# Folding batch 1 by mirrored rows first, and moving its transforms and the channel-128 transform

## The chip, the cores and the metric

The kernel runs on one core of a Trainium2 chip. The metric is the device time of one execution in microseconds (us), as the median over several executions. Engine names in the profile: PE is TensorE (PEld its weight loads), DVE is VectorE, ACT is ScalarE, POOL is GpSimd, SP issues most DMAs.

## The reference

```
X = fft(x, axis=1); X = fft(X, axis=2); a = X.real          # x: (8, 3008, 256), float32
t = a.reshape(24064, 256)
h = t @ w_in                                                # (256, 2048)
g = where(h > 0, h, exp(min(h, 0)) - 1)
out = g @ w_out                                             # (2048, 256)
```

The weights are given as 64-bit floats, which the kernel turns into float32 itself.

## The kernel before

**The Fourier part.** The real part of a two-dimensional transform of real data is symmetric, so only half of the sequence positions of a batch (1504 columns, plus one middle column done apart at the end) and 129 of the 256 channels are needed. The transform along the channels is folded into the weights at the start (`fold_chunk` builds `Wc` and `Ws`). The transform along the sequence is a matmul with constant matrices (`MC` for batches 0 and 1, `QM` for batches 2 to 7). It is run in four parts per batch: `ri` 0 (cosine, result in `Rr`) or 1 (sine, result in `Ir`), and `kodd` 0 or 1 (even or odd output positions, which fill the first or second half, RUN = 752 columns, of the batch's 1504). Each part has two halves `par` of three matmuls that go to a PSUM bank of their own: the even half is copied (`copy`, on ACT) and unfolded (`unfold`, two DVE sums into `bs`); the odd half is added and subtracted (`plus`, `minus`, DVE) and so written into the ring. `Rr`, `Ir` and `Rb` are rings of 2048 columns.

**Folding x.** Ahead of the sequence transform the rows that share a cosine up to sign are added. For batch 1, x comes as four tiles `L[0]` to `L[3]` of 128 partitions x 6 rows x 256 channels; `L[1]` and `L[2]` hold the rows in mirrored order. `fold_x` (L636) first folds the channels of each tile (channel d with channel 256 - d: sum into `e0` to `e3`, difference into `o0` to `o3`), then adds and subtracts these over the tiles, which gives the four inputs `EO` of the transforms. All of it is GpSimd work in 32 operations of 384 columns (and four copies of 6 columns for channel 0), put one or two to a step in the order of `FOLDS`. Batches 2 to 7 do it the other way round: `mirror_sum` and `half_sum` add rows, then `channel_fold` folds the channels.

**Channel 128.** The one channel that the folds leave out is transformed for all eight batches at once. `load_ext` reads it element by element, `get_ext` reads it back from DRAM into `xs`, `fold_ext` (GpSimd) makes `xe`, `dft_ext` (TensorE, 24 short matmuls) transforms it, `ext_side` (ACT) copies the four results from PSUM into `side` tiles, `ext_unfold` and `ext_rows` (DVE, on 8 partitions) add them up into a row tile `rx`, which is written to DRAM (`r128_dr`). `spread_ext` reads a row of it for a batch into all partitions of the ring `Rb` and into row 127 of `Ir`.

**The main loop.** 47 tiles of 256 columns, each in eight steps over the 2048 hidden values: 376 steps. In step n TensorE runs `mm_P` (four instructions of the profile, `H<-Rr,Wc`) and later `mm_Q` (`H<-Ir,Ws`), both into one bank `H`; between them DVE's `even_part` (E, L1193) reads the bank, adding channel 128, so `mm_Q` waits for E. `h_minus` (L1207) makes the mirrored columns' values; ACT makes the negative parts (`below_plus`, `below_minus`) and their exponentials (`exp_plus`, `exp_minus`); `g_plus` and `g_minus` (L1223) finish the activation one step later, and with `g_plus` the bank H is free. There are three banks H. Then GpSimd forms four sums of G (L548, `sum_1` to `sum_4`) and TensorE multiplies by `w_out` with seven products per step (`mm_X1` to `mm_X3`, into `pA` to `pD`), with the weight sums `WT`. Every eighth step the tile's result is combined (`comb_copy` on ACT; `comb_1`, `comb_2`, `comb_22`, `comb_3` on DVE), transposed (`turn_u`, `turn_v`) and stored.

**What sets the order.** Every action is put on a list with a due time, in units of T = 4.8 us per step: `at(33 * T + 1.46, fn)` is 1.46 us after the start of step 33. The list is sorted by these times and run once, and each engine's instructions stay in that order. The times order the instructions; they don't delay them. `at_dft(step, gap, ...)` places a transform: even half at the end of `step` (4.75), unfold in the next step at 1.0, odd half at the end of `step + gap`, ring writes in the step after that at 1.01. DMAs on the SP queue are not pinned to the list and are arranged by the framework; those that GpSimd issues are pinned.

Some lines that the prediction uses are helpers: L539 is every matmul, L545 every DVE sum of two tensors, L548 every GpSimd sum, L551 every ACT operation.

Of the kernel before, what the change touches and what calls it, by code (L numbers as in the profile page):

```python
# [9 lines left out]
FP = mybir.dt.float32  # L10
# [152 lines left out]
def kernel(  # L163
# [466 lines left out]
    def fold_x(L, engine_of, cuts_of):  # L630
# [44 lines left out]
        op("EO3", O[3], O[0], O[2], ALU.add)  # L675
        return [E[1], E[3], O[1], O[3]], ops

    FOLDS = (
        "e0 c0 e3 c3 e2 c2 x1 e1 c1 E0 E2 EO0 o0 o3 o2 o1 O0 O2 EO2 EO1 EO3".split()
    )  # L680

    def lines(j, far):

# [437 lines left out]
    def ext_rows(kodd, tt, rows=NB):  # L1121
        n = NO if kodd else NE
        if not kodd or rows < NB:
            rx = spool.tile([128, HALF + 1], FP, tag="rx", bufs=1, name="rx")
            state["rx"] = rx[0:rows]
        rx, a, b = state["rx"], state["es"], state["side", 1][0:rows]
        o, base = 1 - kodd, kodd * RUN
        m = n - 2 * o
        tt(rx[:, base : base + n], a[:, 0:n], b[:, 0:n], ALU.add)
        top = base + RUN - 1  # L1130
        tt(rx[:, top : top - m : -1], a[:, o : o + m], b[:, o : o + m], ALU.subtract)
        if not kodd:
            tt(rx[:, HALF:], a[:, 0:1], b[:, 0:1], ALU.subtract)
            nc.sync.dma_start(
                out=r4_dr.rearrange("o b -> b o"), in_=rx[:, HALF : HALF + 1]
            )
        nc.sync.dma_start(
            out=r128_dr[0:rows, base : base + RUN], in_=rx[:, base : base + RUN]
        )

    def spread_ext(b, kodd):
        for sl, a, z in ring_cut(b * HALF + kodd * RUN, RUN, False):
# [373 lines left out]
    def at(t, fn):  # L1516
        events.append((t, len(events), fn))
# [248 lines left out]
        at_half(step, d, 0, 0)  # L1766
        at_half(step + gap, d, 1, b * HALF + (kodd + 1) * RUN)

    def begin_folds(b):
        state["EO"], state["ops"] = fold_x(  # L1770
            state["L"], lambda key: nc.gpsimd, lambda key, n: (0, n // 2, n)
        )

    steps_b = HALF * 8 // TW
    at(9 * T + 4.75, dft_ext_0)
# [5 lines left out]
    for n in range(16):  # L1781
# [2 lines left out]
            (14.4 + 0.5 * n) * T,  # L1784
            lambda j=j, k=k: load_ext(j, 192 * k, 192 * (k + 1)),
        )
    at(30.0 * T, get_ext)
    at(32 * T + 1.35, fold_ext)
    at(32 * T + 4.75, dft_ext)
    at(33 * T + 1.46, lambda: ext_side(0))  # L1790
    at(33 * T + 1.47, lambda: ext_side(1))
    at(35 * T + 0.2, lambda: ext_unfold(0, vtt))
    at(35 * T + 1.5, lambda: ext_rows(0, vtt))
    at(35 * T + 4.75, lambda: ext_side(2))
    at(35 * T + 4.76, lambda: ext_side(3))
    at(36 * T + 0.2, lambda: ext_unfold(1, vtt))
    at(36 * T + 1.5, lambda: ext_rows(1, vtt))
    at(27 * T + 4.3, quarter_table)
    at(34 * T, lambda: nc.sync.dma_start(out=twist_tab[0:96], in_=QT_dr.ap()))
    for n in range(4):  # L1800
# [1 line left out]
            (51 + 3 * n) * T,  # L1802
            lambda n=n: load_quarter_mats(n % 2, n // 2),
        )
    fold_keys = [(k, p) for k in FOLDS for p in range(2 if k[0] not in "cx" else 1)]
    first = (6, 7, 7, 8, 9, 9, 10, 10, 12, 15)

    def fold_slot(n):
        return first[n] if n < len(first) else 17 + n - len(first)

    at(fold_slot(0) * T, lambda: begin_folds(1))
    n = 0
    for key in fold_keys:
        slot = fold_slot(n)
        at(
            slot * T + (3.5 if slot < 16 else 1.3),
            lambda key=key: state["ops"][key](),
        )
        n += key[0][0] not in "cx"
    for n, (ri, kodd) in enumerate(((0, 0), (1, 0), (0, 1), (1, 1))):  # L1820
        at_dft(
            (28, 36, 40, 44)[n], 2, 1, ri, kodd, lambda k=2 * ri + kodd: state["EO"][k]
        )
    for kodd, step in ((0, 37), (1, 40)):
        at(step * T + 1.0, lambda kodd=kodd: spread_ext(1, kodd))

    def at_quarter(step, b, ri, kodd, finish, join):
# [24 lines left out]
    for b in range(2, NB):  # L1852
# [4 lines left out]
            at((r0 + step) * T + dt, lambda: fn(*key))  # L1857

        for far, rows in (
            (0, ((0, 2, 0.2), (1, 2, 1.3), (3, 3, 0.2), (2, 3, 1.3))),  # L1860
            (1, ((0, 27, 1.3), (1, 25, 0.2), (3, 28, 1.3), (2, 26, 3.0))),
        ):
            for j, n, dt in rows:
                rel(n, dt, load_quarter, b, j, far)
# [83 lines left out]
```

## Time and profile before

| | |
|---|---|
| median of 3 runs (lowest to highest) | 1920.8 us (1920.65 to 1921.17) |
| the profiled execution: its own time | 1921.02 us |
| its span on the core | 1919.1 us |
| PE busy | 1909.2 us (99%), 9008 instructions |
| DVE busy | 1436.9 us (75%) |
| ACT busy | 872.3 us (45%) |
| POOL busy | 1356.9 us (71%) |
| TensorE clock granted | 1.00 |

How to read it: a float32 matmul stands as two instructions. Matmuls are pipelined, so PE's records overlap: consecutive ones over 256 columns start 0.216 us apart though one lasts 0.38. A step of 22 such instructions takes 4.75 us, and where it takes longer without more matmuls, TensorE has waited. Steps are counted from 0 by their first `H<-Rr,Wc`; step 0 starts at 26.57 us, step 36 at 224.35. In the windows view each row is one stretch of the span, with the busy time of each engine in it. In the timeline a row is one instruction or several alike in sequence, with start and length, and in brackets how long the engine stood idle and what ended that.

### The profile page before, as it was taken

The numbers are of one execution on the slowest core, as the hardware profiler recorded it, in microseconds if no ns is written. First come the engines' busy times: TensorE is split into PE (matmuls) and PEld (weight loads), VectorE is DVE, ScalarE is ACT, GpSimd is POOL, SyncE is SP. The second block draws the span as 40 slices with busy tenths as digits, with TensorE's granted clock in tenths as the row PEclk, the third lists the DMA queues.
The fourth block names the chain that finished last, engine by engine and source line by source line (L and its number), as shares of the span: only waits on it lengthen the run. The fifth ranks groups of instructions, "written<-read, shape, count | busy, mean of one in ns | idle before, by whom it ended". The sixth has DMA issues, their size and how long they took to land.

```text
span 1919.1 us, 27636 instructions
## 1 busy us (share of the span) xinstructions
PE 1909.2 (99%) x9008; PEld 1653.4 (86%) x9008; DVE 1436.9 (75%) x2714; ACT 872.3 (45%) x1710; POOL 1356.9 (71%) x1843
## 2 busy tenths in 40 slices
PE   9999999999999999999999999999999999999999
PEld 6788788888888888888888888888888888888887
DVE  8866767877778777777777777777777777667666
ACT  5654444444444444444444444444444444444443
POOL 4888767786687766777667776687766876556565
PEclk9999999999999999999999999999999999999999
DMA  8146112111011110211101111022110210000101
GB/s 338 44 33 52 35 41 53 40 22 33 12 44 37 27 34 12 51 30 31 26 19 45 34 28 26 12 52 43 25 20 12 53 22 15 16 12 14 21 11 24
DMA packets 271073, 71.88 MB, mean 37 GB/s; under 512 B 256815, under 2 KB 257731, under 8 KB 270929
## 3 DMA queue, kind: packets, MB, share of 16 engines
q1 hardware_dynamic: 257296, 57.34, 15.0%
q0 software_dynamic: 11456, 12.52, 2.2%
q8 instruction: 71, 1.16, 0.3%
q14 instruction: 74, 0.60, 0.1%
q10 hardware_dynamic: 2176, 0.26, 0.1%
HBM read 45.20 MB, written 24.80 MB: 36 GB/s over the span
## 4 chain that ended last, share of the span: by engine, by line
PE 96%; DVE 1%; POOL 1%; ACT 0%; DMA 0%; issue 0%; DVEq 0%; POOLq 0%
PE H L539 38%; PE pB L539 17%; PE pC L539 17%; PE pD L539 16%; PE pA L539 9%; POOL WT L548 1%; DMA xl<-in_x_dram,ix 0%; POOL w L548 0%; DVE e L636 0%; ACT G L551 0%; DVE pow L407 0%; DVE o L636 0%; DVE E L1193 0%; DVE G L1223 0%; DVE G L1207 0%
## 5 line engine op out<-in xcount | busy, mean ns | idle before, releaser
L548 POOL TENSOR_TENSOR G<-G 128x256 f32<-128x256 f32 x1440 | 1045.6, 735 | 508.6 <-DVE G L1223 341.9
L551 ACT ACTIVATE G<-H 128x512 f32<-128x512 f32 x376 | 224.5, 597 | 936.5 <-DVE G L1207 931.7
L1193 DVE SCALAR_TENSOR_TENSOR E<-Rb,wex,H 128x256 f32<-128x256 f32 x752 | 328.0, 477 | 376.7 <-PE H L539 371.9
L539 PE MATMUL H<-Ir,Ws 128*128 128x256 f32 x1504 | 387.2, 380 | 2.0 <-DVE E L1193 2.0
L539 PE MATMUL H<-Rr,Wc 128*128 128x256 f32 x1504 | 387.8, 380 | 0.8 <-DVE Ir L545 0.8
L539 PE MATMUL pC<-G,WT 128*128 128x256 f32 x1440 | 369.5, 379 | 0.0
L539 PEld LDWEIGHTS H<-Ir,Ws 128*128 128x128 f32 x1504 | 278.0, 189 | 51.1 <-DVE E L1193 5.6
L539 PEld LDWEIGHTS H<-Rr,Wc 128*128 128x128 f32 x1504 | 282.1, 190 | 44.1 <-issue 2.2
L539 PEld LDWEIGHTS pC<-G,WT 128*128 128x128 f32 x1440 | 273.6, 190 | 37.2
L1207 DVE SCALAR_TENSOR_TENSOR G<-E,H 128x512 f32<-128x512 f32 x376 | 257.0, 684 | 44.6 <-POOL G L548 11.9
L1223 DVE SCALAR_TENSOR_TENSOR G<-G,H 128x512 f32<-128x512 f32 x376 | 255.9, 681 | 40.1 <-ACT G L551 40.1
L1223 DVE SCALAR_TENSOR_TENSOR G<-M,G 128x512 f32<-128x512 f32 x376 | 256.8, 683 | 0.4 <-ACT M L551 0.4
L551 ACT ACTIVATE G<-G 128x512 f32<-128x512 f32 x376 | 233.4, 621 | 0.0
L539 PE MATMUL pD<-G,w 128*128 128x256 f32 x784 | 229.3, 379 | 0.0
L539 PE MATMUL pB<-G,w 128*128 128x256 f32 x784 | 229.3, 379 | 0.0
L539 PE MATMUL pA<-G,w 128*128 128x256 f32 x784 | 229.3, 379 | 0.0
L551 ACT ACTIVATE M<-G 128x512 f32<-128x512 f32 x376 | 224.3, 596 | 3.1 <-DVE G L1207 3.1
L551 ACT ACTIVATE M<-M 128x512 f32<-128x512 f32 x376 | 221.1, 588 | 0.1
L539 PE MATMUL pB<-G,WT 128*128 128x256 f32 x720 | 214.5, 379 | 0.4 <-POOL G L548 0.3
L539 PE MATMUL pD<-G,WT 128*128 128x256 f32 x720 | 214.1, 379 | 0.0
L539 PEld LDWEIGHTS pA<-G,w 128*128 128x128 f32 x784 | 148.9, 190 | 20.5
L539 PEld LDWEIGHTS pD<-G,w 128*128 128x128 f32 x784 | 149.0, 190 | 20.3
(178 smaller groups left out, 1540.1 us busy)
## 6 DMA issues: line engine op xcount, KB each, us to landing
out_dram<-ot SPq DMA_DIRECT2D x496, 32.0 KB
xq<-in_x_dram SPq DMA_DIRECT2D x12, 384.0 KB
out_dram<-ot SPq DMA_DIRECT2D x256, 2.0 KB
xq<-in_x_dram SPq DMA_DIRECT2D x12, 320.0 KB
Rb<-r SPq DMA_DIRECT2D x10, 376.0 KB
raw<-in_moe_w_in_dram SPq DMA_DIRECT2D x7, 512.0 KB
MC<-dft_mats SPq DMA_DIRECT2D x3, 943.5 KB
xl<-in_x_dram SPq DMA_DIRECT2D x4, 512.0 KB
```

The source lines that it names most:

```text
L539: nc.tensor.matmul(out_, lhsT=lhsT, rhs=rhs, start=start, stop=stop, skip_group_check=True)
L548: pin(nc.gpsimd.tensor_tensor(out=o, in0=a, in1=b, op=op))
L551: pin(nc.scalar.activation(out=o, in_=i, func=func, **kw))
L1193: nc.vector.scalar_tensor_tensor(out=S.E[:, c], in0=Rb[:, cols(i)], scalar=wex[:, f : f + 1], in1=S.H[:, c], op0=ALU.mult, op1=ALU.add,)
L1207: nc.vector.scalar_tensor_tensor(out=two(S.G[:, 0:512])[:, :, ::-1], in0=two(S.E), scalar=2.0, in1=two(S.H), op0=ALU.mult, op1=ALU.subtract,)
L1223: nc.vector.scalar_tensor_tensor(out=o, in0=e, scalar=-1.0, in1=h, op0=ALU.add, op1=ALU.max)
```

## The change

- `mirror_folds` takes the place of `fold_x` for batch 1 (batch 0 still uses `fold_x`). It first adds the mirrored rows in place (`L[3]` with `L[2]`, `L[0]` with `L[1]`; each 6 operations of 255 columns and one of 6), then forms sum and difference of `L[0]` and `L[3]` over the freed tiles `L[1]` (kodd 0) and `L[2]` (kodd 1), 4 operations of 384 columns each, and folds the channels of these two, 4 operations of 384 columns each. That is 30 GpSimd operations in place of 36. Channel 0 comes by one ACT copy per `kodd` (`edge`).
- Two to five folds are put in each of the steps 6 to 9; the last is in step 30, where it was 38. The copy of one row from `L[0]` to `L[1]` on ACT comes in step 7 in place of 10.
- Channel 128: `get_ext`, `fold_ext`, `dft_ext` three steps sooner. The two `ext_side` copies for kodd 0 are in step 30 (before 33), those for kodd 1 in step 33 (before 35). `ext_rows(0)` becomes `ext_up` and `ext_down`; the sums are due at 4.25 of steps 30, 31 and 32 (before 0.2 and 1.5 of step 35), those for kodd 1 at 4.25 of steps 53 and 54 (before 0.2 and 1.5 of step 36). `spread_ext(1, 0)` is in step 33 (before 37), `spread_ext(1, 1)` in step 55 (before 40).
- Batch 1's four transforms start in steps 26, 34, 37, 42 (before 28, 36, 40, 44).
- For batch 2 the first load of `xq2` is in step 31 (before 29), since `L[2]` is in use longer.

```diff
--- before.py
+++ after.py
@@ -675,9 +675,60 @@
         op("EO3", O[3], O[0], O[2], ALU.add)
         return [E[1], E[3], O[1], O[3]], ops
 
-    FOLDS = (
-        "e0 c0 e3 c3 e2 c2 x1 e1 c1 E0 E2 EO0 o0 o3 o2 o1 O0 O2 EO2 EO1 EO3".split()
-    )
+    def mirror_folds(L):
+
+        ops = []
+        rows = [t.rearrange("p (m d) -> p m d", d=ND) for t in L]
+        for j, k in ((3, 2), (0, 1)):
+            own, other = rows[j], rows[k][:, ::-1]
+            for m in range(6):
+                ops.append(
+                    lambda own=own, other=other, m=m: gtt(
+                        own[:, m, 1:], own[:, m, 1:], other[:, m, :0:-1], ALU.add
+                    )
+                )
+            ops.append(
+                lambda own=own, other=other: gtt(
+                    own[:, :, 0:1], own[:, :, 0:1], other[:, :, 0:1], ALU.add
+                )
+            )
+        EO = [None] * 4
+        for kodd in range(2):
+            z = L[1 + kodd]
+            for n in range(4):
+                c = slice(384 * n, 384 * n + 384)
+                ops.append(
+                    lambda z=z, c=c, kodd=kodd: gtt(
+                        z[:, c], L[0][:, c], L[3][:, c],
+                        ALU.subtract if kodd else ALU.add,
+                    )
+                )
+            for ri in range(2):
+                t = EO[2 * ri + kodd] = spool.tile(
+                    [128, 768], FP, tag=f"{'eo'[ri]}{1 + 2 * kodd}", bufs=1, name="eo"
+                )
+                for h in range(2):
+
+                    def fold(z=rows[1 + kodd], t=t, ri=ri, h=h):
+                        src = z[:, 3 * h : 3 * h + 3]
+                        lo, hi = (
+                            v.rearrange("p m (d o) -> p m o d", o=2)
+                            for v in (src[:, :, 1:129], src[:, :, 255:127:-1])
+                        )
+                        o = t[:, 384 * h : 384 * h + 384]
+                        o = o.rearrange("p (m o d) -> p m o d", o=2, d=64)
+                        if ri:
+                            gtt(o, lo, hi, ALU.subtract)
+                        else:
+                            gtt(o, lo[:, :, ::-1], hi[:, :, ::-1], ALU.add)
+
+                    ops.append(fold)
+                if not ri:
+                    o = t.rearrange("p (m o d) -> p m o d", o=2, d=64)
+                    state["edge", kodd] = lambda o=o, z=rows[1 + kodd]: act(
+                        o[:, :, 0, 63:64], z[:, :, 0:1]
+                    )
+        return EO, ops
 
     def lines(j, far):
 
@@ -1137,6 +1188,25 @@
         nc.sync.dma_start(
             out=r128_dr[0:rows, base : base + RUN], in_=rx[:, base : base + RUN]
         )
+
+    def ext_up():
+        rx = state["rx"] = spool.tile(
+            [128, HALF + 1], FP, tag="rx", bufs=1, name="rx"
+        )[0:NB]
+        a, b = state["es"], state["side", 1][0:NB]
+        vtt(rx[:, 0:NE], a, b[:, 0:NE], ALU.add)
+        vtt(rx[:, HALF:], a[:, 0:1], b[:, 0:1], ALU.subtract)
+
+    def ext_down():
+        rx, a, b = state["rx"], state["es"], state["side", 1][0:NB]
+        vtt(
+            rx[:, RUN - 1 : RUN - 1 - (NE - 2) : -1],
+            a[:, 1 : NE - 1], b[:, 1 : NE - 1], ALU.subtract,
+        )
+        nc.sync.dma_start(
+            out=r4_dr.rearrange("o b -> b o"), in_=rx[:, HALF : HALF + 1]
+        )
+        nc.sync.dma_start(out=r128_dr[0:NB, 0:RUN], in_=rx[:, 0:RUN])
 
     def spread_ext(b, kodd):
         for sl, a, z in ring_cut(b * HALF + kodd * RUN, RUN, False):
@@ -1766,10 +1836,9 @@
         at_half(step, d, 0, 0)
         at_half(step + gap, d, 1, b * HALF + (kodd + 1) * RUN)
 
-    def begin_folds(b):
-        state["EO"], state["ops"] = fold_x(
-            state["L"], lambda key: nc.gpsimd, lambda key, n: (0, n // 2, n)
-        )
+    def begin_folds():
+        L = state["L"]
+        state["EO"], state["ops"] = mirror_folds(L)
 
     steps_b = HALF * 8 // TW
     at(9 * T + 4.75, dft_ext_0)
@@ -1784,17 +1853,18 @@
             (14.4 + 0.5 * n) * T,
             lambda j=j, k=k: load_ext(j, 192 * k, 192 * (k + 1)),
         )
-    at(30.0 * T, get_ext)
-    at(32 * T + 1.35, fold_ext)
-    at(32 * T + 4.75, dft_ext)
-    at(33 * T + 1.46, lambda: ext_side(0))
-    at(33 * T + 1.47, lambda: ext_side(1))
-    at(35 * T + 0.2, lambda: ext_unfold(0, vtt))
-    at(35 * T + 1.5, lambda: ext_rows(0, vtt))
-    at(35 * T + 4.75, lambda: ext_side(2))
-    at(35 * T + 4.76, lambda: ext_side(3))
-    at(36 * T + 0.2, lambda: ext_unfold(1, vtt))
-    at(36 * T + 1.5, lambda: ext_rows(1, vtt))
+    at(27.0 * T, get_ext)
+    at(29 * T + 1.35, fold_ext)
+    at(29 * T + 4.75, dft_ext)
+    at(30 * T + 1.46, lambda: ext_side(0))
+    at(30 * T + 1.47, lambda: ext_side(1))
+    at(30 * T + 4.25, lambda: ext_unfold(0, vtt))
+    at(31 * T + 4.25, ext_up)
+    at(32 * T + 4.25, ext_down)
+    at(33 * T + 1.46, lambda: ext_side(2))
+    at(33 * T + 1.47, lambda: ext_side(3))
+    at(53 * T + 4.25, lambda: ext_unfold(1, vtt))
+    at(54 * T + 4.25, lambda: ext_rows(1, vtt))
     at(27 * T + 4.3, quarter_table)
     at(34 * T, lambda: nc.sync.dma_start(out=twist_tab[0:96], in_=QT_dr.ap()))
     for n in range(4):
@@ -1802,26 +1872,21 @@
             (51 + 3 * n) * T,
             lambda n=n: load_quarter_mats(n % 2, n // 2),
         )
-    fold_keys = [(k, p) for k in FOLDS for p in range(2 if k[0] not in "cx" else 1)]
-    first = (6, 7, 7, 8, 9, 9, 10, 10, 12, 15)
-
-    def fold_slot(n):
-        return first[n] if n < len(first) else 17 + n - len(first)
-
-    at(fold_slot(0) * T, lambda: begin_folds(1))
-    n = 0
-    for key in fold_keys:
-        slot = fold_slot(n)
+    first = (6, 6, 7, 7, 7, 7, 7, 8, 8, 8, 9, 9, 9, 9, 12, 15)
+
+    at(6 * T, begin_folds)
+    at(7 * T + 3.4, lambda: act(state["L"][1][0:1, 5 * ND :], state["L"][0][0:1, 0:ND]))
+    for n in range(30):
+        slot = first[n] if n < len(first) else n + 1
         at(
             slot * T + (3.5 if slot < 16 else 1.3),
-            lambda key=key: state["ops"][key](),
+            lambda n=n: state["ops"][n](),
         )
-        n += key[0][0] not in "cx"
-    for n, (ri, kodd) in enumerate(((0, 0), (1, 0), (0, 1), (1, 1))):
-        at_dft(
-            (28, 36, 40, 44)[n], 2, 1, ri, kodd, lambda k=2 * ri + kodd: state["EO"][k]
-        )
-    for kodd, step in ((0, 37), (1, 40)):
+    for kodd, slot in ((0, 20), (1, 28)):
+        at(slot * T + 4.0, lambda kodd=kodd: state["edge", kodd]())
+    for step, ri, kodd in ((26, 0, 0), (34, 1, 0), (37, 0, 1), (42, 1, 1)):
+        at_dft(step, 2, 1, ri, kodd, lambda k=2 * ri + kodd: state["EO"][k])
+    for kodd, step in ((0, 33), (1, 55)):
         at(step * T + 1.0, lambda kodd=kodd: spread_ext(1, kodd))
 
     def at_quarter(step, b, ri, kodd, finish, join):
@@ -1857,7 +1922,7 @@
             at((r0 + step) * T + dt, lambda: fn(*key))
 
         for far, rows in (
-            (0, ((0, 2, 0.2), (1, 2, 1.3), (3, 3, 0.2), (2, 3, 1.3))),
+            (0, ((0, 2, 0.2), (1, 2, 1.3), (3, 3, 0.2), (2, 5 if b == 2 else 3, 1.3))),
             (1, ((0, 27, 1.3), (1, 25, 0.2), (3, 28, 1.3), (2, 26, 3.0))),
         ):
             for j, n, dt in rows:
```

## The prediction

> **What bounds the kernel now.** I read the page's busy shares first, then its chain, then the windows step by step, and last the timeline where steps are too long.
>
> ```profile
> PE 1909.2 (99%) x9008; PEld 1653.4 (86%) x9008; DVE 1436.9 (75%) x2714; ACT 872.3 (45%) x1710; POOL 1356.9 (71%) x1843
> PE 96%; DVE 1%; POOL 1%; ACT 0%; DMA 0%; issue 0%; DVEq 0%; POOLq 0%
> ```
>
> TensorE is busy all the time and is the chain. The change removes no matmul (the program's TensorE list has 4312 rows before and after), so it can only win back TensorE's waits. To see those I cut the span where each step's first `H<-Rr,Wc` starts, since a pipelined busy figure hides short waits:
>
> ```profile
> core 0: us, PE busy (x) PEld busy (x) DVE busy (x) ACT busy (x) POOL busy (x), PEclk, DMA share, GB/s
> ...
> 180.16:186.19 6.03, 6.03 (x30) 5.18 (x28) 3.57 (x7) 2.81 (x6) 5.59 (x7) 1.00 0.64 72
> ...
> 209.20:214.05 4.85, 4.85 (x24) 4.26 (x23) 2.35 (x5) 2.32 (x5) 3.22 (x6) 1.00 0.31 90
> 214.05:218.53 4.48, 4.17 (x20) 3.23 (x19) 4.38 (x9) 2.12 (x4) 4.32 (x7) 1.00 0.00 0
> 218.53:224.35 5.82, 5.77 (x27) 4.72 (x26) 5.82 (x11) 2.12 (x4) 4.36 (x7) 1.00 0.01 2
> 224.35:232.52 8.17, 6.64 (x29) 5.12 (x29) 7.48 (x13) 3.91 (x8) 6.79 (x9) 1.00 0.23 38
> ...
> 248.67:254.94 6.27, 6.27 (x29) 5.11 (x28) 4.14 (x7) 3.20 (x6) 5.82 (x9) 1.00 0.01 1
> ...
> 293.24:298.19 4.95, 4.95 (x24) 4.10 (x22) 4.87 (x9) 2.80 (x6) 4.58 (x7) 1.00 0.00 0
> 298.19:302.94 4.75, 4.75 (x24) 4.16 (x23) 3.75 (x7) 2.25 (x6) 3.28 (x6) 1.00 0.00 0
> 302.94:306.82 3.88, 3.88 (x19) 3.40 (x18) 3.67 (x8) 1.71 (x4) 2.99 (x4) 1.00 0.14 22
> 306.82:312.43 5.61, 5.61 (x27) 4.94 (x26) 4.24 (x8) 3.08 (x7) 5.09 (x7) 1.00 0.16 55
> ```
>
> A plain step takes 4.75 us. One followed by the even half of a transform takes 6.03 (step 28, first row), so that half costs 1.28. The rows from 209.20 are steps 33 to 36, then 40, then 48 to 51. Against undisturbed steps of their kind:
> - Steps 33 to 35 take 4.85 + 4.48 + 5.82 = 15.15, where 49 to 51 take 4.75 + 3.88 + 5.61 = 14.24: 0.91 over. 0.10 of it is the change of shape after the narrow channel-128 matmuls. Lost: 0.81.
> - Step 36: 8.17 - 6.03 = 2.14.
> - Step 40: 6.27 - 6.03 = 0.24. Step 48: 4.95 - 4.75 = 0.20.
>
> Together 3.39 us. No other step from 18 to 60 is long. The timeline names the holders:
>
> ```profile
> 216.70 1.13 PE L539 MATMUL H<-Ir,Ws 128*128 128x256 f32 x4 [0.31 <-DVE E L1193]
> ...
> 221.30 2.31 DVE L545 TENSOR_TENSOR rx<-bs,side 8x377 f32<-8x377 f32 x3
> ...
> 223.54 0.67 DVE L1223 SCALAR_TENSOR_TENSOR G<-G,H 128x512 f32<-128x512 f32 x1
> ...
> 226.62 0.70 PE L539 MATMUL pB<-G,WT 128*128 128x256 f32 x2 [0.30 <-POOL G L548]
> ...
> 227.64 0.85 DVE L1193 SCALAR_TENSOR_TENSOR E<-Rb,wex,H 128x256 f32<-128x256 f32 x2
> ...
> 228.54 1.13 PE L539 MATMUL H<-Ir,Ws 128*128 128x256 f32 x4 [1.23 <-DVE E L1193]
> ```
>
> In steps 35 and 36 the channel-128 sums (`rx<-bs,side`, `bs<-side`) stand between `even_part` and `g_plus`. VectorE is then full (5.82 of 5.82, 7.48 of 8.17): `g_plus` gives its PSUM bank back at 224.21, just before step 36's first matmul, the E that `mm_Q` needs comes 1.23 late, and the G sums on GpSimd make one product wait. The first row is another loss: in step 34 `mm_Q` waits for an E queued behind two combination sums.
>
> **What the Trainium skill says.** "TensorE: Matmul & The Clock Gate" (The mechanism): matmuls start and end in program order. The trace agrees: no later matmul passes the one waiting until 228.54, so a late input costs its whole wait. "SBUF — State Buffer" (Who interferes with whom): a VectorE operation with two SBUF inputs contends with a GpSimd operation that reads SBUF. The trace agrees: `rx<-bs,side` over 377 columns takes 1.25 us on 8 partitions, where `Rr<-bs,H`, one input in PSUM, takes 0.54 on 128. I therefore price moved sums at contended durations.
>
> **The change, part by part.**
> 1. *Channel-128 sums.* In quiet steps (30, 38) VectorE runs E from 1.06 to 1.94 us after the step's start, `g_plus` to 2.53, `g_minus` to 3.14, `h_minus` 3.28 to 3.97. The next E is due at 4.75 + 1.06 = 5.81, so the pause is 1.84. Contended prices from steps 35 and 36: step 30 gets the unfold, 1.30; step 31 gets 1.25 + 0.14 (no overlap) = 1.39; step 32 gets 1.06; step 53 gets 1.14 to 1.30; step 54 gets 1.54 to 1.60. All fit with 0.24 or more to spare; the two half sums of step 46, 1.37 long, sit in the same place without loss. Cost 0, and none of it has further cover: past 5.81 each us is a us on TensorE. Removing them from 35 and 36 gives back 2.14 and the 0.21 that step 36's first matmul waited for its bank: **-2.35**.
> 2. *The ACT copies.* `ext_side(0)` and `(1)`, 0.95, move to step 30, behind a transform of 2.1 us; ACT is idle there. `ext_side(2)` and `(3)`, 0.98, come to 33T + 1.46, exactly where 0 and 1 were, behind `comb_copy`, which waits for TensorE until 1.60. So `exp_plus`, `g_plus`, `h_minus` and the two combination sums run as late as now, and step 34's wait stays: **0** gained of its 0.58. Were the copies free there: -0.58; if more is late: +0.3.
> 3. *Transforms.* Their matmuls cost the same wherever they stand. The ring writes (1.06 to 1.13 us) leave step 39 for 37, and 47 for 45, so `h_minus` ends at 3.97 instead of 4.70 ahead of the half sums, and these no longer push E in steps 40 and 48: **-0.44**. In 37, 40 and 45 the writes end `h_minus` by 4.8, as in 31 now, with nothing behind them.
> 4. *GpSimd.* Out: 16 folds from x (10.0 + 9.4 us), 16 pair folds (8.1 + 8.0), 4 copies (1.0), 36.5 in all. In: 12 mirrored sums at 0.735 (the row `xq<-xq,xq`) 8.8, two edges 0.4, 8 sums at about 1.0, 8 folds at about 1.2, together 26.8. Its relief in steps 31 to 38 is what lets the G sums be early; TensorE's 0.57 for that wait is already inside the 2.14. In steps 7 to 9 it carries up to 1.2 us more than now, but its weight pairs are finished some 4 us ahead of `fold_chunk`, and it idles 0.88 at 97.08: 0, bounds -0.3 and +0.5. The two edges on ACT (6 columns) have no row; the nearest is the copy of the same shape on GpSimd, 0.24: idle ACT hides it, at worst +0.3.
> 5. *Queues.* On SP the three early and one late reads of `xs` now go ahead of or around the `xq0` load, which waits for GpSimd's last use of `xl0` in step 26. The last read is issued at 182.84 now. GpSimd needs it at step 29 + 2.0, which is near 190 (step 29 begins 1.9 later than now, with 3.2 of transforms before it instead of 1.3). 2048 packets at the present rate need some 3 us: about 4 us of slack, cost 0. The indirect load of `xq2` on the POOL queue moves from step 29 to 31; 0.94 of issue either way, landing in 4 to 5 us there now, read two steps later. Had it the 11.5 us of other stages, GpSimd would wait 1.5 and TensorE up to 1. The row writes and broadcasts run three steps sooner for half 0 and at step 55 for half 1, needed in 40 and 64.
>
> Sum: -2.35 - 0.44 = -2.79. The profiled execution took 1921.02 (span 1919.1), so 1918.2; the median of the runs is 0.2 lower, 1920.8, so 1918.0. For tenths lost anew I take 0.1 back: **1918.1**. That is 0.14%, inside the 0.2% (3.8 us) a measurement of this kernel can tell from no change.
>
> **Rivals.**
> - *The pauses are too short.* For: margins of 0.24 to 0.8, and contended durations scatter (0.55 to 0.95 for one half sum). Against: the half sums fit. If the five steps each push E by 0.4 plus 0.1 of restart, 2.5 comes back: 1920.4.
> - *GpSimd waits for channel 128* (the slower case). If the last read lands late, `fold_ext` blocks GpSimd at step 29 and four G sums queue behind it, for which TensorE waits. The sums have about 2 us to spare, so it decides from a landing near 192 on, one us for each us. Slower by 0.2% takes 2.8 + 3.8 = 6.6 us more, near 199. For: single-element packets fill the DMA engines until about 178 (share 0.7 to 1.07). Against: two loads of 384 KB leave that stretch. At a landing near 200: 1925.5.
> - *Step 34's wait goes too*, and the 0.36 at 134.3 where GpSimd's weights are late: 1917.2.
> - *Nothing moves*, because the instruction order stayed: excluded for VectorE, whose list has the sums in 30 to 32 and 53 to 54; if the waits have another cause, 1920.8.
>
> **How the numbers follow.** Forecast case, 1917.4 to 1918.9: 0.65. Short pauses or an unmoved wait, 1918.9 to 1920.9: 0.20. Step 34 too: 0.05. Slower: 0.10, nearly all past 0.2%. Range 1917.2 to 1920.6. Faster by over 0.2% means below 1917.0; the 3.39 found plus 0.36 come to 3.75, just short of it, so 0.03. Slower 0.09, same 0.88.
>
> **What would show it.** Right: step 36's `H<-Ir,Ws` has no wait, the first matmul of step 36 follows at once, steps 40 and 48 take their kind's time, while `H<-Ir,Ws` of step 34 still waits 0.3 for E. Wrong: waits of TensorE for E in steps 31 to 33 or 54 to 55, for G sums in 29 to 31 (then look at `xs`), or a stretch before 140 us that has changed by over half a us.

## The result, and the profile after

The changed kernel takes **1918.03 us** (median of 22 runs, 1917.18 to 1919.11), where the kernel before takes 1920.80 (22 runs on the same chip). The ratio is 0.9985, with a 95% interval of 0.9979 to 0.9992. So it is faster by 2.8 us, 0.14%, less than the 0.2% that the prediction set as its bound.

One step boundary after the other, the two profiled executions differ like this:

| stretch | before, us | after, us | difference |
|---|---|---|---|
| start to step 18 | 132.31 | 131.60 | -0.71 |
| steps 18 to 59 | 218.10 | 215.41 | **-2.69** |
| steps 60 to 374 | 1550.98 | 1550.87 | -0.11 |
| from step 375 | 17.72 | 17.61 | -0.11 |

Together that is 3.62 of span (1919.1 to 1915.5), and 3.76 of time (1921.02 to 1917.26). The profiled execution of the changed kernel is one of its fastest, 0.8 below its median; that of the kernel before is 0.2 above its own. The difference of the medians is 2.77, so the first row needs care; it comes back at the end of the experiments. Its 0.25 before step 0 is no gain: among the profiles of all runs step 0 starts anywhere from 26.0 to 26.8.

The page's busy shares and its chain have hardly moved, except that TensorE's share is now rounded to 100%:

```profile
PE 1908.1 (100%) x9008; PEld 1654.2 (86%) x9008; DVE 1433.0 (75%) x2714; ACT 872.7 (46%) x1712; POOL 1349.7 (70%) x1837
PE 97%; POOL 1%; DVE 1%; DMA 0%; ACT 0%; issue 0%; DVEq 0%; POOLq 0%
```

The instructive view is again the windows by step, of the changed kernel. The rows are steps 30, 33 to 36, 40 and 48:

```profile
core 0: us, PE busy (x) PEld busy (x) DVE busy (x) ACT busy (x) POOL busy (x), PEclk, DMA share, GB/s
...
194.22:199.07 4.85, 4.85 (x25) 4.26 (x23) 3.54 (x7) 2.80 (x6) 3.01 (x4) 1.00 0.14 21
...
208.56:213.31 4.75, 4.75 (x23) 4.16 (x22) 2.20 (x5) 2.79 (x6) 2.40 (x5) 1.00 0.42 105
213.31:219.21 5.90, 5.59 (x25) 4.19 (x24) 5.36 (x10) 2.53 (x5) 4.67 (x8) 1.00 0.19 61
219.21:224.82 5.61, 5.61 (x27) 4.94 (x26) 3.90 (x8) 2.67 (x7) 4.24 (x7) 1.00 0.00 0
224.82:231.48 6.66, 6.66 (x30) 5.30 (x29) 3.38 (x6) 3.50 (x7) 4.86 (x7) 1.00 0.32 54
...
248.89:253.63 4.74, 4.74 (x23) 4.15 (x22) 3.58 (x7) 0.07 (x1) 1.16 (x2) 1.00 0.32 92
...
290.04:294.79 4.75, 4.75 (x24) 4.16 (x23) 4.03 (x8) 2.12 (x5) 3.80 (x6) 1.00 0.00 0
```

Step 36 now carries the odd half of a transform, which costs 1.90 (steps 28 and 39 of the same kind take 6.65 too), and loses nothing: its PE column is as long as the row. VectorE, which filled 5.82 and 7.48 us in steps 35 and 36, is busy for 3.90 and 3.38. Steps 40 and 48 take their plain 4.75. Step 30 has the 0.10 of the change of shape after the narrow matmuls, which step 33 had before. The one step from 19 to 59 that still waits is 34. It should take 3.88 + 1.28 (the even half that now follows it) = 5.16 and takes 5.90: 0.74 lost, where it lost 0.60 before.

The sums now lie where the prediction put them. This is VectorE's timeline of the changed kernel in steps 30 to 32, which start at 194.22, 199.07 and 203.82:

```profile
198.20 1.22 DVE L545 TENSOR_TENSOR bs<-side 8x189 f32<-8x189 f32 x2
200.13 0.87 DVE L1263 SCALAR_TENSOR_TENSOR E<-Rb,wex,H 128x256 f32<-128x256 f32 x2 [0.71 <-PE H L539]
...
202.95 1.22 DVE L545 TENSOR_TENSOR rx<-bs,side 8x377 f32<-8x377 f32 x2
204.88 0.87 DVE L1263 SCALAR_TENSOR_TENSOR E<-Rb,wex,H 128x256 f32<-128x256 f32 x2 [0.71 <-PE H L539]
...
207.70 0.60 DVE L545 TENSOR_TENSOR rx<-bs,side 8x375 f32<-8x375 f32 x1
```

After each sum E begins 1.06 after its step's start, and VectorE has stood idle for 0.71 before it, waiting for TensorE and not the reverse. And this is the loss that stayed, in the timeline of step 34 (starts at 213.31; the first two rows are the ACT copies and the exponential of step 33):

```profile
210.46 0.98 ACT L551 ACTIVATE side<-H 8x376 f32<-8x376 f32 x2
211.34 0.61 ACT L551 ACTIVATE G<-G 128x512 f32<-128x512 f32 x1
...
211.99 0.69 DVE L1293 SCALAR_TENSOR_TENSOR G<-G,H 128x512 f32<-128x512 f32 x1 [1.48 <-ACT G L551]
...
214.58 0.69 DVE L545 TENSOR_TENSOR v<-u,pC 128x512 f32<-128x512 f32 x1
...
215.18 0.86 DVE L1263 SCALAR_TENSOR_TENSOR E<-Rb,wex,H 128x256 f32<-128x256 f32 x2
...
216.10 1.13 PE L539 MATMUL H<-Ir,Ws 128*128 128x256 f32 x4 [0.31 <-DVE E L1263]
```

It is a chain of five links: the copies `side<-H` hold back the exponential on ACT, this holds back `g_plus` (1.48 idle), so all later VectorE work of step 33 is late, the combination sums run into step 34, E follows them without a pause, and TensorE waits for E.

### The profile page after: what moved, and what is told of

Same layout as the page of the kernel before. It is cut to its first block, busy times and chain, and to the rows that moved or that the text cites. A ratio compares the mean times of both kernels' runs of the same rounds, so it can differ in the third digit from the quotient of the medians.

```text
span 1915.5 us, 27634 instructions
## 1 busy us (share of the span) xinstructions
PE 1908.1 (100%) x9008; PEld 1654.2 (86%) x9008; DVE 1433.0 (75%) x2714; ACT 872.7 (46%) x1712; POOL 1349.7 (70%) x1837
## 4 chain that ended last, share of the span: by engine, by line
PE 97%; POOL 1%; DVE 1%; DMA 0%; ACT 0%; issue 0%; DVEq 0%; POOLq 0%
PE H L539 38%; PE pB L539 17%; PE pC L539 17%; PE pD L539 17%; PE pA L539 9%; POOL WT L548 1%; DMA xl<-in_x_dram,ix 0%; DVE e L636 0%; POOL w L548 0%; DVE o L636 0%; POOL G L548 0%; POOL xl L548 0%; PE M L539 0%; DVE v L545 0%; ACT G L551 0%
## 5 line engine op out<-in xcount | busy, mean ns | idle before, releaser
L539 PEld LDWEIGHTS pB<-G,w 128*128 128x128 f32 x784 | 148.9, 190 | 20.4 <-PE H L539 0.2
```

Of the source, the lines that this page charges most:

```text
L539: nc.tensor.matmul(out_, lhsT=lhsT, rhs=rhs, start=start, stop=stop, skip_group_check=True)
```

## The experiments

Unless said otherwise "steps 18 to 59" is the length of that stretch in the profiled execution (218.10 before, 215.41 after), and each run's ratio is to the kernel before on the same chip (1920.8 to 1921.02). The changed kernel, run again beside some of them, took 1917.92.

### Which part of the change is worth what

**The second half's sums alone.** The kernel before, with only these moved:

```diff
-    at(36 * T + 0.2, lambda: ext_unfold(1, vtt))
-    at(36 * T + 1.5, lambda: ext_rows(1, vtt))
+    at(53 * T + 4.25, lambda: ext_unfold(1, vtt))
+    at(54 * T + 4.25, lambda: ext_rows(1, vtt))
-    for kodd, step in ((0, 37), (1, 40)):
+    for kodd, step in ((0, 37), (1, 55)):
```

> The kernel before, with one change: the channel-128 sums of the second half are due at 4.25 of steps 53 and 54 instead of 0.2 and 1.5 of step 36, and spread_ext of that half follows in step 55. Folds, transforms and the first half stay. Theory 1 (step 36 loses its time to its own sums): the wait of H<-Ir,Ws in step 36 (1.39 with its restart) goes, what is left there is the 0.3 to 0.6 for the bank and for G: 1919.2 us, steps 18 to 60 in 216.5 us. Theory 2 (the sums of step 35 keep E of step 36 late anyhow): 1920.3 or above, 217.5 us or more.

It took 1919.25 (13 runs, 1918.96 to 1919.69; ratio 0.9992, interval 0.9984 to 1.0001), steps 18 to 59 in 216.55. The row of step 36 in the windows, and the waits that the timeline of TensorE still names in steps 34 to 36:

```profile
224.55:231.22 6.67, 6.37 (x28) 5.19 (x29) 4.93 (x9) 4.18 (x8) 6.43 (x9) 1.00 0.26 43
```

```profile
216.90 1.13 PE L539 MATMUL H<-Ir,Ws 128*128 128x256 f32 x4 [0.32 <-DVE E L1193]
226.82 0.70 PE L539 MATMUL pB<-G,WT 128*128 128x256 f32 x2 [0.30 <-POOL G L548]
```

Step 36 falls from 8.17 to 6.67. The wait of 1.23 for E is gone, and what is left is what the first half's sums in step 35 leave behind: 0.28 for the bank at the step's first matmul (0.21 of it in step 35's row) and 0.57 for a G sum. A bracket says less than a wait costs: it counts from the end of the record before, which lasts 0.38 where the next could start after 0.216, so 0.16 more is lost; and the second matmul after a wait starts 0.32 later instead of 0.216, 0.10 more. 0.30 in the bracket is 0.57 of loss, and the 1.23 were 1.49. So these two edits are worth 1.5 of the 2.8 us, and step 36 lost its time to its own sums. The interval of the ratio includes 1 (its end is 1.0001); it is the trace that places the gain. Not all of the 1.49 was the length of the sums. In the kernel before, the unfold of step 36 also waited for the ACT copies that it reads, and E stood behind it:

```profile
226.56 1.14 DVE L545 TENSOR_TENSOR bs<-side 8x188 f32<-8x188 f32 x2 [0.54 <-ACT side L551]
```

**The fold alone.** `mirror_folds`, its slots and the later load of `xq2` are put into the kernel before, with the transforms in 28, 36, 40 and 44 and channel 128 where it was:

```diff
-    for step, ri, kodd in ((26, 0, 0), (34, 1, 0), (37, 0, 1), (42, 1, 1)):
+    for step, ri, kodd in ((28, 0, 0), (36, 1, 0), (40, 0, 1), (44, 1, 1)):
...
+    at(35 * T + 0.2, lambda: ext_unfold(0, vtt))
+    at(35 * T + 1.5, lambda: ext_rows(0, vtt))
```

> The mirrored-row fold alone: transforms in steps 28, 36, 40, 44 and the channel-128 work at the old times. Theory 1 (the place of the channel-128 sums in steps 35 and 36 costs the time; GpSimd's relief alone cannot move E of step 36): step 36 still takes about 8.1 us; 1920.0 to 1920.8, less only by what the start gives (step 12, 0.57 in the one profile). Theory 2 (GpSimd was the cause, its folds in steps 29 to 38 made the G sums late and contended with VectorE's sums): step 36 falls to near 6.1; 1918.5.

It took 1920.76 (13 runs, 1919.80 to 1922.83; ratio 1.0, interval 0.9991 to 1.0008). Its profiled execution, 1919.80, is its fastest; steps 18 to 59 take 217.27 in it. There the waits for G and for the bank are gone, and E's is not; step 36 takes 7.58, between the 8.1 and the 6.1 of the two theories:

```profile
223.20:230.78 7.58, 6.36 (x29) 5.04 (x28) 6.35 (x12) 4.26 (x8) 5.41 (x9) 1.00 0.23 39
```

```profile
226.81 1.13 PE L539 MATMUL H<-Ir,Ws 128*128 128x256 f32 x4 [1.22 <-DVE E L1263]
```

The row sums of step 35 took 1.51 there instead of 2.31. But the fold alone gains nothing that the runs can show. The 0.83 of its profiled execution is more than its median supports (0.26 below the kernel before on that chip, with runs that scatter over 3 us), and I don't use it.

**The old fold in the changed kernel.** `mirror_folds` is taken out again (`fold_x` and its 36 operations in the old slots), and all else stays as changed.

> Changed kernel, but batch 1 folded in the old way, in 36 GpSimd operations up to step 38. Theory 1: VectorE's places give the time, so steps 33 to 48 stay as in the changed kernel apart from at most 0.6 of waits for G sums; step 12 loses its 0.57 again; 1918.0 to 1919.0. Theory 2: GpSimd is over-full in steps 29 to 38 again, and 2 us or more come back: 1920 or more.

It took 1918.21 (21 runs, 1917.67 to 1919.58; ratio 0.9986, interval 0.9979 to 0.9992), steps 18 to 59 in 215.45: within 0.04 of the changed kernel. With the rest moved, the new fold is not needed for the gain in these steps. In steps 29 to 38 no TensorE wait for a G sum came back either, although GpSimd has its old load.

**The later transforms back.** The three later transforms are put back:

```diff
-    for step, ri, kodd in ((26, 0, 0), (34, 1, 0), (37, 0, 1), (42, 1, 1)):
+    for step, ri, kodd in ((26, 0, 0), (36, 1, 0), (40, 0, 1), (44, 1, 1)):
```

> Changed kernel with the last three transforms of batch 1 at their old steps (36, 40, 44; the first stays in 26). My theory (ring writes in steps 39 and 47 end h_minus late, ahead of half sums that then push E in 40 and 48): steps 40 and 48 take 6.27 and 4.95 again, 0.44 more, 1918.5. Rival (those two were after-effects of the crowded steps 35 and 36): both stay undisturbed, 1918.0.

It took 1918.65 (21 runs; ratio 0.9988, interval 0.9981 to 0.9994), steps 18 to 59 in 215.91, which is 0.50 more than as changed. Steps 40 and 48 are long again, to within a hundredth, and make 0.43 of it:

```profile
246.02:252.29 6.27, 6.27 (x29) 5.11 (x28) 4.14 (x7) 3.20 (x6) 5.82 (x9) 1.00 0.01 1
...
290.59:295.53 4.94, 4.94 (x23) 4.10 (x22) 4.86 (x9) 2.79 (x6) 4.57 (x7) 1.00 0.00 0
```

**Step 34's wait.** In the changed kernel the two copies are put after the exponentials of step 33:

```diff
-    at(33 * T + 1.46, lambda: ext_side(2))
-    at(33 * T + 1.47, lambda: ext_side(3))
+    at(33 * T + 2.3, lambda: ext_side(2))
+    at(33 * T + 2.31, lambda: ext_side(3))
```

> Changed kernel, with ext_side(2) and (3) due at 33T + 2.3 instead of 33T + 1.46, so that ACT does exp_plus and exp_minus of the step first. My theory (the two copies of 0.98 us ahead of exp_plus make g_plus, h_minus and the two combination sums late, and step 34's H<-Ir,Ws waits for E): that matmul no longer waits, 0.57 us less, 1917.4. Rival (the two combination sums alone are what is in E's way): nothing changes, 1918.0, and step 34 still takes 5.90.

It took 1917.34 (14 runs, 1916.50 to 1917.89; ratio 0.9981, interval 0.9973 to 0.9989), 0.6 below the changed kernel's repeat. Steps 18 to 59 take 214.74, which is 0.67 less: step 34 gives back 0.74, and step 18 takes 0.07 more. The copies stand behind the exponential, `g_plus` doesn't wait for them, and step 34 takes its 5.16:

```profile
210.99 0.62 ACT L551 ACTIVATE G<-G 128x512 f32<-128x512 f32 x1
...
212.12 0.98 ACT L551 ACTIVATE side<-H 8x376 f32<-8x376 f32 x2
```

```profile
213.97:219.13 5.16, 5.16 (x25) 4.42 (x24) 4.44 (x9) 2.18 (x5) 3.82 (x6) 1.00 0.04 14
```

That confirms the chain, whose first link was taken out: a place in ACT's queue, on an engine that is 46% busy, was worth 0.7 us of TensorE.

### Is it the pauses that count, or something else?

The prediction held that a sum costs nothing only in a pause behind `h_minus`. Four runs test this.

**All first-half sums in one pause.**

```diff
-    at(30 * T + 4.25, lambda: ext_unfold(0, vtt))
+    at(31 * T + 4.24, lambda: ext_unfold(0, vtt))
     at(31 * T + 4.25, ext_up)
-    at(32 * T + 4.25, ext_down)
+    at(31 * T + 4.26, ext_down)
```

> Changed kernel with all sums of channel 128's first half (unfold, up, down) in the one pause of step 31. By the trace they take 2.9 us together, from 3.88, so they end near 6.8, where E of step 32 is due at 5.81. Theory 1 (a pause is 1.9 us long and each us past it is a us on TensorE, less the 0.22 that H<-Ir,Ws has to spare): step 32 longer by 0.75 to 0.9, about 1918.9. Theory 2 (VectorE makes it up within the step): 1918.0.

It took 1919.03 (20 runs; ratio 0.999, interval 0.9984 to 0.9997), steps 18 to 59 in 216.62: 1.2 more than as changed. VectorE in steps 31 and 32, then TensorE:

```profile
203.34 1.22 DVE L545 TENSOR_TENSOR bs<-side 8x189 f32<-8x189 f32 x2
204.59 2.03 DVE L545 TENSOR_TENSOR rx<-bs,side 8x377 f32<-8x377 f32 x3
206.55 0.85 DVE L1263 SCALAR_TENSOR_TENSOR E<-Rb,wex,H 128x256 f32<-128x256 f32 x2
```

```profile
207.46 1.13 PE L539 MATMUL H<-Ir,Ws 128*128 128x256 f32 x4 [0.93 <-DVE E L1263]
```

Step 32 starts at 204.21, so E begins at 2.34 instead of 1.06: 1.28 late, for which step 32 takes 1.2 longer. A pause holds what the prediction said and not more; beyond it a us of VectorE is nearly a us of TensorE. I had expected 0.75 to 0.9: the sum over 377 columns took 0.97 here.

**Sums outside the pauses, but sooner.** The changed kernel, with the sums at the places within the step that they had before (ahead of `g_plus`), in steps 32 and 33 instead of 35 and 36:

```diff
-    at(30 * T + 4.25, lambda: ext_unfold(0, vtt))
-    at(31 * T + 4.25, ext_up)
-    at(32 * T + 4.25, ext_down)
-    at(33 * T + 1.46, lambda: ext_side(2))
...
-    at(53 * T + 4.25, lambda: ext_unfold(1, vtt))
-    at(54 * T + 4.25, lambda: ext_rows(1, vtt))
+    at(32 * T + 0.2, lambda: ext_unfold(0, vtt))
+    at(32 * T + 1.5, lambda: ext_rows(0, vtt))
+    at(32 * T + 4.75, lambda: ext_side(2))
...
+    at(33 * T + 0.2, lambda: ext_unfold(1, vtt))
+    at(33 * T + 1.5, lambda: ext_rows(1, vtt))
```

> Changed kernel with channel 128 three steps sooner, but its sums at the old places within a step (unfold at 0.2 of steps 32 and 33, rows at 1.5, the late ACT copies at 4.75 of step 32). Theory 1 (the place within the step is what counts): steps 32 to 34 become long as 35 and 36 were, 2 to 3.5 us more than the changed kernel, 1920.0 to 1921.5. Theory 2 (being away from steps 35 and 36, where two transposes stand, is what counts): at most 0.7 more, 1918.7.

It took 1918.15 (20 runs; ratio 0.9986, interval 0.9980 to 0.9993), steps 18 to 59 in 215.86. My theory fell: I had expected 2 to 3.5 us more, and it is 0.45 in the trace. Step 33 loses 1.04, because E stands behind the second unfold. That one didn't run long; it waited for the ACT copies that it reads:

```profile
209.71 1.14 DVE L545 TENSOR_TENSOR bs<-side 8x188 f32<-8x188 f32 x2 [1.16 <-ACT side L551]
```

Against that, the copies run 1.3 earlier in step 33 than in the changed kernel and no longer hold up its `g_plus`, and step 34 loses 0.14 instead of 0.74. So the 0.45 is a loss of 1.04 and a gain of 0.60, and it says little about the place of the sums alone. Then **the first half alone outside its pauses**, with the second in 53 and 54 and the copies after the exponentials:

```diff
-    at(30 * T + 4.25, lambda: ext_unfold(0, vtt))
-    at(31 * T + 4.25, ext_up)
-    at(32 * T + 4.25, ext_down)
+    at(32 * T + 0.2, lambda: ext_unfold(0, vtt))
+    at(32 * T + 1.5, lambda: ext_rows(0, vtt))
```

> The kernel of e1_sides_after_exp, but the channel-128 sums of the first half are not spread over three pauses: the unfold stands in the pause of step 31 and the two row sums are put together between E and g_plus of step 32, as they stood in step 35 before; the sums of the second half stay in steps 53 and 54. Theory 1 (where GpSimd is lightly loaded the sums run at 0.5 to 0.7 us each and their place within a step costs nothing): as e1, 1917.3 us, steps 18 to 60 in 214.6 to 215.0 us. Theory 2 (a sum ahead of g_plus costs TensorE something everywhere): step 32 or 33 gets a wait for E of 0.3 or more, steps 18 to 60 in 215.1 or more, 1917.7 or above.

It took 1917.12 (16 runs; ratio 0.9982, interval 0.9974 to 0.9989), steps 18 to 59 in 214.71, as with the pauses (1917.34 and 214.74). Both row sums stand between E and `g_plus` here and TensorE loses nothing. So why did the same sums at the same place hurt so much in step 35? The run that tells is **the old fold with the sums outside the pauses**: the kernel of 1918.15 with `fold_x` instead of `mirror_folds`.

> The kernel of e5_old_places_sooner (channel 128 sooner, its sums in steps 32 and 33 at the places within the step that they have in the kernel before), but batch 1 folded as in the kernel before, one fold to a step. It tells whether the new fold is what made the sums cheap there. Theory 1 [...]: the sums over 377 columns take 1.0 to 1.3 us instead of 0.54, E of step 33 is later, TensorE waits 1 us more there: 1919.2 us, steps 18 to 60 in some 216.8 us. Theory 2 (the distance from steps 35 and 36, where a transform's writes also stand, is all that matters): as e5, 1918.2 us, 215.9 us.

It took 1919.74 (12 runs, 1918.86 to 1920.05; ratio 0.9994, interval 0.9985 to 1.0002), steps 18 to 59 in 217.24: 1.4 more than with the new fold, where I had expected 1. VectorE's sums and what GpSimd does beside them, in step 32, first with the old fold:

```profile
206.43 1.86 DVE L545 TENSOR_TENSOR rx<-bs,side 8x377 f32<-8x377 f32 x3
```

```profile
205.82 1.01 POOL L636 TENSOR_TENSOR o<-o,o 128x384 f32<-128x384 f32 x1
206.78 1.51 POOL L548 TENSOR_TENSOR xq<-xq,xq 96x255 f32<-96x255 f32 x2
```

and with the new fold:

```profile
205.70 1.06 DVE L545 TENSOR_TENSOR rx<-bs,side 8x377 f32<-8x377 f32 x3
```

```profile
204.77 0.88 POOL L548 TENSOR_TENSOR xq<-xq,xq 96x255 f32<-96x255 f32 x2
207.50 3.15 POOL L548 TENSOR_TENSOR G<-G 128x256 f32<-128x256 f32 x4 [1.85 <-DVE G L1293]
```

The same three sums take 1.86 us beside GpSimd's work and 1.06 where GpSimd stands idle. With the old fold GpSimd is at work from before the first of them until the last ends; with the new one it has 1.85 us of idle time just there. These 0.80 are passed on: `h_minus`, the ACT copies, the second unfold and E of step 33 all come 0.80 later in their steps, and step 33 takes 6.59 instead of 5.79. The other 0.56 of the 1.4 is in step 34 (5.86 against 5.30), behind row sums that took 1.55 instead of 0.99. The four runs make a square:

| sums of channel 128 | old fold | new fold |
|---|---|---|
| in pauses | 1918.21 (215.45) | 1918.03 (215.41) |
| ahead of `g_plus`, steps 32 and 33 | 1919.74 (217.24) | 1918.15 (215.86) |

(median time, and steps 18 to 59, us.) The rows can be read as they stand: in the pauses the fold makes no difference, ahead of `g_plus` it is worth 1.4. The columns can't, since the ACT copies of kodd 1 also stand elsewhere in the lower row. So take what steps 33 and 34 lose against undisturbed ones (4.75 and 5.16): in the pauses 0.75 with the old fold and 0.74 with the new, which is the wait of step 34 that the place of the copies causes; ahead of `g_plus` 2.54 with the old fold and 1.18 with the new. With the copies after the exponentials and the sums in pauses it is 0 with the new fold (with the old one that was not run).

So the pauses are enough with either fold, and the lighter GpSimd alone takes away about half of the loss. The pauses take the sums out of the way of E and `g_plus`; the lighter GpSimd makes the row sums shorter. What is left with the new fold comes with the second half's sums and their copies, since the first half's alone cost nothing in the same place; whether earlier copies would remove it was not tried.

### Step 12, and the best version

The first row of the table in the result was not predicted. Of its 0.71 us, 0.57 are in step 12, 0.25 are the earlier step 0, and 0.12 is lost in step 6, which takes 9.24 in all profiles with the new fold and 9.12 in those with the old. The timeline of VectorE and GpSimd in step 10 shows where the 0.57 come from. `pow<-raw,pow` (a part of the weights' conversion) has two inputs in SBUF. First the kernel before:

```profile
90.15 1.28 POOL L548 TENSOR_TENSOR w<-raw,w 128x512 f32<-128x512 f32 x1
90.75 1.25 DVE L407 SCALAR_TENSOR_TENSOR pow<-raw,pow 128x512 int32<-128x512 int32 x1
```

The changed kernel:

```profile
90.60 0.68 DVE L407 SCALAR_TENSOR_TENSOR pow<-raw,pow 128x512 int32<-128x512 int32 x1
```

```profile
90.60 1.26 POOL L548 TENSOR_TENSOR xl<-xl,xl 128x255 f32<-128x255 f32 x1
```

And the version with the copies after the exponentials, whose program is the same up to this point:

```profile
90.62 1.24 DVE L407 SCALAR_TENSOR_TENSOR pow<-raw,pow 128x512 int32<-128x512 int32 x1
```

```profile
90.59 0.73 POOL L548 TENSOR_TENSOR xl<-xl,xl 128x255 f32<-128x255 f32 x1
```

Whoever starts first takes its short time, and the other takes 0.53 to 0.57 longer. "SBUF — State Buffer" (Who interferes with whom) says: "Issue order, not op shape, decides who blocks." These rows agree. In the four profiles with the old fold, GpSimd's operation is 0.59 to 0.61 us ahead and `pow` is always long. In the nine with the new fold and without a later edit here, a GpSimd sum starts within 0.04 us of `pow`: four times VectorE was first, five times GpSimd. So the change turned a certain loss into a toss. In all thirteen profiles step 12 takes 7.03 to 7.06 us where `pow` is long and 6.48 or 6.49 where it is short. TensorE pays through E of step 12, which begins at 101.47 in the version with the copies after the exponentials and at 100.88 in the changed kernel. First the former, then the latter:

```profile
102.39 1.13 PE L539 MATMUL H<-Ir,Ws 128*128 128x256 f32 x4 [0.50 <-DVE E L1263]
```

```profile
101.80 1.13 PE L539 MATMUL H<-Ir,Ws 128*128 128x256 f32 x4
```

**The best of the edits together**: the copies after the exponentials, and a fold moved from step 15 to 12, which takes away TensorE's wait for GpSimd's first sums of G near 134 (0.35 us in all).

```diff
-    first = (6, 6, 7, 7, 7, 7, 7, 8, 8, 8, 9, 9, 9, 9, 12, 15)
+    first = (6, 6, 7, 7, 7, 7, 7, 8, 8, 8, 9, 9, 9, 9, 12, 12)
```

> Changed kernel with two moves: the late ACT copies after exp_minus of step 33 (as before, 0.7 less), and the fold of step 15 put in step 12, where GpSimd idles for 3 us before the weight sums. Theory: GpSimd's unbroken stretch from 114 us to the first G sums is 1.0 shorter, so the wait of 0.23 and 0.10 at 133.6 goes; 1917.0. Rival (that wait comes from elsewhere, the G of VectorE): as with the copies alone, 1917.3.

It took 1916.84 (11 runs, 1915.77 to 1917.31; ratio 0.9977, interval 0.9968 to 0.9986). On the same chip the changed kernel was run again:

> The changed kernel unaltered, for its profile and as the mark for the others on this chip. If step 12's 0.57 is decided by which of VectorE and GpSimd starts first at 90.6 us in the single execution, step 12 takes 6.48 or 7.05 here, with the sum of step 10 on VectorE at 0.68 or 1.24 us; if it were the change's own doing, 6.48. Median 1918.0.

It took 1917.92 (19 runs, 1917.44 to 1918.64; ratio 0.9984, interval 0.9977 to 0.9991). So the two edits are worth 1.1 us; steps 18 to 59 fell by 1.09 as well (215.43 to 214.34), which is 0.75 in step 34 and 0.35 in step 18.

**A loaded toss.** To that version one thing is added: a mirrored sum of step 9 is cut in two, so that GpSimd's next one starts later.

```diff
+                cuts = (1, 128, ND) if (j, m) == (0, 3) else (1, ND)
+
+                def mirror(own=own, other=other, m=m, cuts=cuts):
+                    for a, z in zip(cuts, cuts[1:]):
+                        gtt(
+                            own[:, m, a:z], own[:, m, a:z],
+                            other[:, m, ND - a : ND - z : -1], ALU.add,
+                        )
```

> The kernel of e9_best with one thing added: one mirrored sum of step 9 (255 columns) is done in two pieces of 127 and 128, so that GpSimd's later sums begin some 0.1 to 0.2 us later. Theory 1 (the sum pow<-raw,pow in step 10 is a race: with the new fold a GpSimd sum begins within 0.03 us of it, and where GpSimd is first VectorE waits for it and takes 1.25 instead of 0.68, so that TensorE loses 0.57 two steps later): VectorE is now first in each execution, pow takes 0.68, step 12 takes 6.48 instead of 7.04, and the time is 0 to 0.6 below e9_best (1916.84), about 1916.5. Theory 2 (the long sum has another cause, or the later GpSimd chain is what holds step 12): pow takes 1.2 or step 12 stays at 7.0, 1916.8 or above.

It took **1916.44** (11 runs, 1916.02 to 1917.94; ratio 0.9977, interval 0.9968 to 0.9986), 0.4 below the version without it. VectorE is first, by 0.12 us, and GpSimd waits:

```profile
90.92 0.71 DVE L407 SCALAR_TENSOR_TENSOR pow<-raw,pow 128x512 int32<-128x512 int32 x1
```

```profile
91.04 1.17 POOL L548 TENSOR_TENSOR xl<-xl,xl 128x255 f32<-128x255 f32 x1
```

Step 12 takes 6.50: one operation more on a busy engine took a wait from TensorE. The trace shows that for one execution; that it is always so is inferred from the margin. The times alone don't show it: the two medians come from two chips, and the intervals of the two ratios are the same.

## Why the prediction was right, and where not

The forecast was 1918.1, and 1918.03 was measured. By its own steps:

1. *Channel-128 sums, -2.35.* Right in place and size: step 36 lost 2.14 and loses 0, and its first matmul follows at once. The runs divide it: 1.5 goes with the second half's sums, the rest with the first half's. The single durations were not right: in the pauses `rx<-bs,side` took 0.62 and 0.60 over 377 and 375 columns against 1.25 and 1.06, but 0.67 over one column against 0.14, and step 54's two took 1.62 against 1.60 at most. Each pause still had room. With the old fold in the changed kernel the first two took 0.96 and 1.18, nearer the price. That a us past the pause is a us of TensorE is shown by the run with one pause: 1.28 late, 1.2 lost.
2. *ACT copies, 0 of step 34's 0.58.* Right: the wait stayed. Step 34 lost 0.14 more than before (0.74 against 0.60), inside the bound of +0.3. Moving the copies behind the exponential gave back the whole 0.74; the bound of -0.58 had been read from the kernel before.
3. *Transforms, -0.44.* Right: steps 40 and 48 are back to their kind, and putting the transforms back restores both rows (0.43; 0.50 in all).
4. *GpSimd, 0.* The 0 was right for steps 18 to 59, the argument was not. The prediction said that GpSimd's relief is what lets the G sums be early. With the old fold in the changed kernel no wait for G appears, so moving the work of steps 35 and 36 is enough. What the relief does is shorten VectorE's two-input sums, which matters only where these stand ahead of `g_plus` or E. It was also smaller than summed: the folds take 29.0 in the trace against 26.8 (a mirrored sum 0.89 on the average against 0.735), where the old ones took 36.6. And the start, bounded at -0.3 to +0.5, loses 0.12 in step 6, and can gain 0.57 in an execution through a collision in step 10 that was not looked for. A stretch before 140 us changing by over half a us was named as a sign against the prediction; it occurred in the profiled execution. It didn't spoil the forecast, because only some executions have it.
5. *Queues, 0.* Right: `fold_ext` ran at 188.0 without waiting; the last read of `xs` had been issued at 182.7 and takes 2.3 at most in the profile, so some 3 us were left of the 4 that were estimated. In 180 to 300 us the list of waits has only one of TensorE, the 0.3 of step 34.

The sum -2.79 stands against -2.69 in steps 18 to 59: -2.14, -0.21, -0.44 and the +0.14 of step 34 make -2.65, and 0.04 is 0.03 in step 18 and rounding. The 0.1 taken back for tenths lost anew named no place; step 34 came near it by chance. The measured medians differ by 2.77. If the toss in step 12 gives half of 0.57 on the average and step 6 takes 0.12, 2.69 becomes some 2.85; runs of one kernel scatter by over a us, so the rest can't be assigned.

Two readings of the prediction don't hold. It says that no other step from 18 to 60 is long, but step 18 takes 4.25 where its kind takes 3.88: it is the 0.36 at 134.3 of its third rival. And five pushes of 0.5 on top of 1918.1 are 1920.6, not 1920.4. Neither touches the forecast.

Of the rivals, the pauses were not too short (steps 31 to 33, 54 and 55 take their 4.75), GpSimd did not wait for channel 128, and step 34's wait did not go by itself. The range from 1917.2 to 1920.6 holds all but one of the 22 runs of the changed kernel.

## What to carry to other kernels

When TensorE is the chain, cut the trace at a matmul that recurs in each step and compare steps of one kind: three us in 1920 show as long rows, and the order of VectorE's and ACT's queues in them says what to move. An operation costs nothing in a pause of its engine only while it ends before the next due one, and its length depends on what GpSimd reads at that time, so there are two remedies. Here the pause was enough alone and the lighter GpSimd was not. A square of four runs tells that, but check first that its rows and columns differ in nothing else. A profile is one execution: where two engines start within hundredths of a us of each other, look at several before a difference is put down to the change.

## What the runs showed of the hardware

- A VectorE operation with two SBUF inputs and a GpSimd sum that overlap act as if they ran one after the other: `pow<-raw,pow` over 512 columns 0.68 or 1.25, the GpSimd sum beside it 1.26 or 0.73, by an order that less than 0.04 us decides. It tosses a whole 0.57 us between executions, and TensorE pays for it two steps later.
- The length of a sum on only 8 partitions is affected as much: three sums over 377, 375 and 1 columns took 1.06, 1.51, 1.86 or 2.31 us in different kernels, with GpSimd idle at 1.06 and at work for most or all of the time at 1.86 and 2.31. Even the sum of one column took 0.14 or, beside GpSimd's sums of G, 0.67.
- A wait of TensorE costs more than itself: the second matmul after one starts 0.32 us later instead of 0.216, in each of the waits looked at.
